# A written order placed anew: the last w_out quarter is loaded ahead of the third batch's x

## The chip, the cores and the metric

The kernel runs on one core of a Trainium2 chip. The metric is the device time of one execution in microseconds (us). Of the kernel before there are three timed runs and one further execution with the hardware profiler, whose trace is read here. In the profile the engines are PE (matrix engine; PEld is its weight load), DVE (vector), ACT (scalar), POOL (GpSimd) and SP (sync, which here only issues DMAs). Each engine works through its own queue in order.

## The reference, cut to what matters

There are 8 batches. Each has x of 8 heads, 512 tokens and depth 64, and a state of 8 heads, 32 rows and depth 64. Two softmax reads are made of the same scores, and their rows go through a two-layer net with a PReLU between.

```
scores = scale * x @ state.T            # [512, 32] per batch and head
xread  = softmax(scores) @ state        # each token reads the states
sread  = softmax(scale * state @ x.T) @ x   # each state row reads the tokens
rows   = concat(xread, sread), heads side by side     # [8 * 544, 512]
h      = rows @ w_in                    # w_in [512, 2048]
g      = max(h, 0) + alpha * min(h, 0)
out    = g @ w_out                      # w_out [2048, 512]
```

## The kernel before, in words

The two matmuls for xread are merged: state @ w_in is formed first (`m`, 32 steps), and h is the softmax weights times that product. So xread itself is never written.

The order of all work on all engines is one list of steps, ORDER (lines 17 to 102). Line 603 goes through the list, and each step appends its instructions to the queues of its engines. A step's letters name it, then follow batch, index, buffer or engine (a = ACT, v = DVE, p = POOL). The steps that the change and the prediction speak of are these:

- `lx.b` (line 162): POOL issues the load of batch b's x into one of four buffers xg. `lx0.g` loads half of batch 0. `lst` loads the states.
- `wi.f` (line 197) and `wo.i` (line 203): POOL issues the load of a quarter of w_in or w_out, 512 KB as written. All these loads turn float32 into float16 and share one software DMA queue.
- `xt`, `xo`: x of batches 0 and 1 is transposed on PE and copied out. `xd.b` (line 269): from batch 2 on, SP issues a DMA transpose of x, from xg to xT; SP waits for the landing of `lx.b` first. `str`, `sro`: states transposed and copied out.
- `sc.b` (line 291): scores on PE, 16 small matmuls, from xT into the PSUM buffer "two". `sb`, `smax`, `ssh`, `sexp`, `ssum`, `snorm`, `wb`: the softmax over states, on DVE, DVE, POOL, ACT, DVE, POOL and DVE; `wb.b` gives the weights aT.
- `tm`, `te`, `tsum`, `tn.b.g`, `tt.b`: the softmax over tokens, on DVE, ACT, DVE, POOL, and a DMA transpose issued by SP. `rd.b`: the state reads on PE, 32 small matmuls that read xg.
- `m.b.f`: state of batch b times w_in quarter f on PE (8 matmuls), into "two", or into two PSUM banks if two numbers follow. `mo`: its two copies to SBUF.
- `F.b.j.k`: h of column block j (16 of them) on PE, two matmuls of 512 columns into PSUM bank k; `f` is one of the two alone. It reads aT and the `m` of quarter j / 4. `N.b.j`: ACT forms max(-h, 0). `G.b.j`: DVE forms g from N and h, and frees the bank. `F.8` stands for the state reads of all batches, four matmuls of 256 columns.
- `S.b.q.i`: two of the 16 matmuls of an output tile q, with g of blocks 2i and 2i + 1; a last number is the PSUM bank. It needs w_out quarter i / 2. `O.b.q.e`: copy out and the store, issued by SP. `R`, `RO`, `L`, `LO` are the same for the state rows and for the last tile, cut into three pieces.
- `Z.k.n`: n matmuls of zeros, whose result is not used.

Of the kernel before, what the change touches and what calls it, by code (L numbers as in the profile page):

```python
# [42 lines left out]
O.1.2.a lx.4 mo.2.2.a.1 sb.3 N.2.15 S.1.0.1 tm.3 F.2.13.3 N.2.13 G.2.15 S.1.0.2 F.2.4.2 tn.2.0
F.2.2.4 G.2.13 smax.3 N.2.4 F.2.9.5 F.2.0.1 N.2.9 S.1.0.3 S.1.0.4 G.2.9 S.1.0.5 N.2.2 N.2.0 te.3.0
F.2.12.3 S.1.0.6 N.2.12 G.2.2 G.2.4 G.2.0 xd.4 F.2.7.5 G.2.12 S.1.3.0.4 ssh.p.3 sexp.3 N.2.7 ssum.3
S.1.0.7 te.3.1 F.2.3.2 S.1.3.1 F.2.1.1 N.2.3 S.1.3.2 N.2.1 F.2.8.3 G.2.3 S.1.3.3 G.2.1 S.1.3.4
S.1.3.5 N.2.8 S.1.3.6 G.2.7 F.2.6.2 O.1.0.a N.2.6 m.3.3.1.0 G.2.8 sc.4 rd.1.5 snorm.p.3 F.2.5.3
G.2.6 mo.3.3.a.0 F.2.14.1 rdo.1.a wb.3 N.2.5 tsum.3 S.2.1.0.2 F.2.11.5 mo.3.3.a.1 G.2.5 S.1.3.7
N.2.14 F.2.10.0 F.3.4.3 G.2.14 N.2.11 S.2.1.1 F.3.1.1 lx.5 O.1.3.v N.3.4 S.2.1.2 N.2.10 G.2.11 tt.2
S.2.0.0.4 S.2.1.3 S.2.0.1 G.2.10 F.3.14.5 F.3.9.0 S.2.1.4 tn.3.1 N.3.1 N.3.9 G.3.1 S.2.1.5 S.2.0.2  # L50
G.3.4 tn.3.0 N.3.14 tm.4 F.3.3.1 F.3.8.3 G.3.14 N.3.8 G.3.9 S.2.1.6 S.2.1.7 S.2.0.3 S.2.3.0.5 N.3.3
xd.5 O.2.1.a tt.3 sb.4 G.3.8 smax.4 F.3.6.0 F.3.2.2 te.4.0 S.2.3.1 S.2.3.2 N.3.6 N.3.2 F.3.13.3
S.2.0.4 te.4.1 ssh.p.4 N.3.13 G.3.3 G.3.6 S.2.0.5 F.3.7.1 G.3.2 S.2.0.6 N.3.7 S.2.0.7 sexp.4 G.3.13
G.3.7 S.2.3.3 S.2.3.4 S.2.3.5 m.6.0 O.2.0.v m.5.1.0.2 mo.6.0.a.1 mo.5.1.a.1 rd.3.3 mo.6.0.v.0
rdo.3.a mo.5.1.v.0 rd.2.1 m.4.1.4.2 ssum.4 sc.5 m.4.3.0.3 rdo.2.a S.2.3.6 mo.4.1.a.1 mo.4.1.a.0 tm.5
tsum.4 snorm.p.4 F.3.5.1 mo.4.3.a.0 mo.4.3.a.1 F.3.0.2 F.3.10.4 N.3.0 S.2.3.7 O.2.3.a S.2.2.0.0
S.2.2.1 F.3.11.3 G.3.0 wb.4 S.2.2.2 S.3.3.0.5 F.3.15.2 S.3.3.1 N.3.5 lx.6 G.3.5 te.5.0 te.5.1 N.3.10
N.3.15 S.2.2.3 F.3.12.1 S.2.2.4 N.3.11 S.3.3.2 lx.7 N.3.12 G.3.10 G.3.15 F.4.6.4 N.4.6 tn.4.0
F.4.5.2 G.3.11 F.4.3.3 N.4.5 S.2.2.5 G.3.12 G.4.5 S.3.3.3 F.4.4.1 S.3.3.4 F.4.7.2 N.4.4 S.3.3.5
S.2.2.6 N.4.3 sb.5 N.4.7 S.3.3.6 S.2.2.7 G.4.4 G.4.7 S.3.3.7 F.4.1.1 F.4.0.2 xd.6 O.2.2.a S.3.1.0.0  # L60
O.3.3.a S.3.1.1 F.4.9.5 N.4.1 smax.5 G.4.6 N.4.0 S.3.0.0.4 tn.4.1 S.3.0.1 G.4.1 G.4.0 F.4.8.1
S.3.1.2 tsum.5 N.4.9 ssh.p.5 G.4.3 sexp.5 N.4.8 G.4.9 F.4.11.2 F.4.2.3 N.4.2 S.3.0.2 ssum.5 S.3.0.3
S.3.0.4 tt.4 N.4.11 S.3.1.3 G.4.8 S.3.1.4 S.3.1.5 G.4.2 S.3.1.6 snorm.p.5 m.5.0.5.1 G.4.11 sc.6
m.5.3.3.2 xd.7 wb.5 mo.5.0.a.1 sb.6 S.3.1.7 mo.5.3.a.0 mo.5.0.a.0 F.4.13.1 N.4.13 S.3.0.5 mo.5.3.a.1
S.3.2.0.3 tm.6 S.3.0.6 te.6.0 F.4.10.5 F.5.3.2 smax.6 S.3.2.1 N.4.10 N.5.3 S.3.2.2 S.3.2.3 S.3.0.7
S.3.2.4 S.3.2.5 S.3.2.6 ssh.p.6 G.4.13 O.3.1.a tn.5.0 F.4.14.1 te.6.1 O.3.0.v S.3.2.7 G.4.10 G.5.3
N.4.14 F.4.12.0 G.4.14 O.3.2.a sexp.6 tn.5.1 S.4.1.0.4 m.6.3 m.7.2.5.2 m.5.2.3.1 mo.6.3.v.0 S.4.1.1
mo.5.2.v.0 mo.7.2.a.0 S.4.1.2 mo.5.2.a.1 F.5.15.5 mo.6.3.v.1 mo.7.2.a.1 tt.5 S.4.1.3 N.5.15 G.5.15
F.4.15.3 F.5.12.1 S.4.1.4 F.5.5.2 N.4.12 F.5.13.5 S.4.1.5 N.5.12 N.4.15 G.4.12 tsum.6 G.4.15
S.4.0.0.0 S.4.1.6 S.4.1.7 N.5.5 S.4.0.1 S.4.2.0.3 O.4.1.v G.5.5 S.4.0.2 F.5.10.4 N.5.13 F.5.1.2  # L70
S.4.2.1 G.5.12 F.5.0.1 N.5.10 S.4.0.3 S.4.2.2 S.4.0.4 G.5.13 tn.6.1 N.5.0 G.5.10 N.5.1 G.5.1
m.6.1.5.4 m.7.0 mo.6.1.a.1 mo.6.1.a.0 S.4.0.5 mo.7.0.v.0 S.4.0.6 F.5.2.2 N.5.2 S.4.0.7 mo.7.0.v.1
G.5.0 O.4.0.a rd.4.4 rd.5.5 G.5.2 m.7.3.1.0 rdo.4.a m.6.2.2.4 sc.7 rdo.5.a ssum.6 mo.7.3.a.0
mo.6.2.a.0 snorm.p.6 tn.6.0 S.4.3.0.5 S.4.3.1 mo.7.3.v.1 F.5.11.1 S.4.3.2 sb.7 S.4.3.3 N.5.11 G.5.11
F.5.6.2 F.5.9.0 S.4.2.3 S.4.2.4 F.5.7.1 S.4.3.4 mo.6.2.a.1 F.5.8.4 smax.7 S.4.3.5 S.4.3.6 wb.6
S.4.3.7 S.4.2.5 N.5.9 N.5.8 N.5.7 G.5.9 O.4.3.a G.5.8 F.5.4.0 N.5.4 tt.6 S.5.0.0.4 S.5.2.0.5 S.4.2.6
G.5.7 G.5.4 F.5.14.1 S.5.2.1 tm.7 S.5.0.1 N.5.6 S.4.2.7 F.6.3.0 N.5.14 G.5.6 S.5.2.2 S.5.0.2 te.7.1
F.6.15.2 N.6.3 G.6.3 S.5.2.3 N.6.15 S.5.2.4 S.5.0.3 G.6.15 ssh.p.7 S.5.2.5 F.6.7.0 S.5.1.0.2 N.6.7
S.5.0.4 G.5.14 O.4.2.v S.5.1.1 F.6.6.1 G.6.7 F.6.8.3 te.7.0 S.5.1.2 N.6.6 S.5.1.3 sexp.7 F.6.1.0
tsum.7 N.6.8 N.6.1 G.6.6 S.5.2.6 F.6.0.1 S.5.0.5 tn.7.1 tn.7.0 S.5.0.6 G.6.8 S.5.2.7 F.6.10.3 tt.7  # L80
N.6.0 S.5.1.4 G.6.1 S.5.1.5 S.5.1.6 S.5.1.7 F.6.14.0 N.6.10 O.5.1.a ssum.7 G.6.10 S.5.0.7 F.6.5.3
snorm.p.7 F.6.2.2 N.6.14 N.6.5 G.6.0 S.5.3.0.1 O.5.0.v G.6.14 m.7.1 G.6.5 rd.7.4 rd.6.0 rdo.7.v
N.6.2 O.5.2.a F.6.13.3 S.5.3.1 mo.7.1.v.0 rdo.6.a S.5.3.2 S.5.3.3 mo.7.1.v.1 F.6.9.5 F.8.4.4 N.6.9
G.6.2 S.5.3.4 wb.7 F.6.12.0 G.6.9 F.6.4.2 N.6.13 N.6.12 S.5.3.5 G.6.12 N.6.4 S.5.3.6 S.5.3.7
S.6.0.0.5 S.6.0.1 N.8.4 F.6.11.0 G.6.13 G.6.4 F.8.10.3 N.6.11 S.6.0.2 N.8.10 O.5.3.v G.8.4 S.6.1.0.2
F.7.0.1 S.6.0.3 F.7.7.4 N.7.0 S.6.1.1 G.6.11 S.6.0.4 N.7.7 S.6.0.5 G.7.0 S.6.1.2 F.8.14.0 S.6.1.3
S.6.1.4 G.8.10 S.6.0.6 N.8.14 F.7.3.1 S.6.0.7 G.7.7 S.6.1.5 F.8.3.3 F.7.6.4 G.8.14 N.7.3 F.8.2.0
O.6.0.v G.7.3 F.7.2.5 F.8.9.1 S.6.1.6 N.8.3 G.8.3 S.6.2.0.3 N.8.2 N.7.2 S.6.2.1 G.8.2 S.6.2.2 N.7.6
# [547 lines left out]
```

## Time and profile before

| what | value |
|---|---|
| three timed runs | 218.6, 218.71, 219.0 us, median 218.71 |
| profiled execution, its own time | 219.66 us |
| its span, first to last instruction | 217.9 us |
| mean granted clock of PE in it | 1.000 |
| PE busy | 210.6 us, 97% of the span |
| DVE busy | 165.2 us, 76% |
| ACT busy | 137.4 us, 63% |
| POOL busy | 71.0 us, 33% |
| software DMA queue (the loads) | 8.62 MB |
| hardware DMA queue (transposes and stores) | 14.23 MB |

A group line of the profile gives line, engine, operation, what is written from what, the count, then the busy time and mean duration, then the idle time of the engine ahead of the group and what ended it. A line of the timeline gives the start in us from the span's start, the duration, the engine and the operation; the bracket tells of idle time just before. "DMA to landing" is the time from a DMA's issue to the signal that all of it has arrived. Matmuls overlap, so one that lasts 379 ns starts 216 ns after the one ahead of it.

### The profile page before, as it was taken

How to read it: one execution, taken by the hardware profiler on the slowest of the kernel's cores; microseconds unless marked ns; L12 is line 12 of the kernel's file. 1: busy time of each engine (PE TensorE's matmuls, PEld its weight loads, DVE VectorE, ACT ScalarE, POOL GpSimd, SP SyncE). 2: the span in 40 equal slices, each digit the busy share in tenths (PEclk: the TensorE clock that was granted, in tenths of full speed). 3: DMA queues.
4: the chain of work that ended last, by engine and by line, in shares of the span. 5: the costliest groups of instructions: out<-in, count | busy, mean ns of one | idle time of the engine just before them, and what ended most of it. 6: DMA issues, size and time to landing. Idle time of an engine off the chain costs nothing.

```text
span 217.9 us, 4311 instructions
## 1 busy us (share of the span) xinstructions
PE 210.6 (97%) x1698; PEld 104.2 (48%) x1698; DVE 165.2 (76%) x250; ACT 137.4 (63%) x271; POOL 71.0 (33%) x58
## 2 busy tenths in 40 slices
...
GB/s 69 188 199 206 200 171 117 206 196 113 92 143 100 92 245 101 51 88 187 249 55 99 96 48 53 0 99 48 50 148 3 46 48 51 48 33 15 51 96 144
DMA packets 41748, 23.12 MB, mean 106 GB/s; under 512 B 24192, under 2 KB 38016, under 8 KB 41728
## 3 DMA queue, kind: packets, MB, share of 16 engines
q0 software_dynamic: 12704, 8.62, 28.5%
q1 hardware_dynamic: 26960, 14.23, 27.7%
q10 hardware_dynamic: 2064, 0.01, 0.5%
q8 instruction: 13, 0.21, 0.4%
q14 instruction: 7, 0.06, 0.1%
...
## 4 chain that ended last, share of the span: by engine, by line
PE 84%; DMA 9%; DVE 3%; POOL 1%; issue 1%; ACT 0%; POOLq 0%
PE o L526 47%; PE h L474 23%; DMA xT<-xg 4%; DMA w_in_sb<-in_moe_w_in_dram 3%; PE m_ps L441 3%; PE h L483 3%; PE o L574 3%; DMA xg<-in_x_dram 2%; PE o L546 2%; PE sr_ps L416 2%; PE sc L291 1%; POOL an L352 1%; DVE ts L326 1%; DVE m L463 1%; DVE mx L332 1%
## 5 line engine op out<-in xcount | busy, mean ns | idle before, releaser
L526 PE MATMUL o<-w_out_sb,gt 128*128 128x512 f16 x496 | 125.3, 379 | 0.9 <-DMA w_out_sb<-in_moe_w_out_dram 0.9
L506 ACT ACTIVATE neg<-h 128x512 f32<-128x512 f32 (+1 forms) x144 | 77.1, 579 | 47.8 <-PE h L474 38.4
L514 DVE SCALAR_TENSOR_TENSOR gt<-neg,oma_sb,h 128x512 f16<-128x512 f32 x128 | 89.9, 738 | 16.5 <-ACT neg L506 15.6
L526 PEld LDWEIGHTS <-gt 128*128 128x128 f16 x496 | 47.3, 98 | 56.4 <-issue 4.5
L474 PE MATMUL h<-aT,m 128*128 128x512 f16 x250 | 68.3, 379 | 0.0
L474 PEld LDWEIGHTS <-m 128*128 128x128 f16 x250 | 24.1, 98 | 28.4 <-issue 0.6
L397 POOL TENSOR_SCALAR e<-e,r 128x512 f16<-128x512 f16 x16 | 25.0, 1566 | 20.4 <-DVE r L393 16.6
L463 ACT CAST m<-m_ps 128x512 f16<-128x512 f32 x50 | 27.1, 606 | 4.6 <-PE m_ps L441 4.3
L352 POOL TENSOR_TENSOR an<-ts,r 128x1024 f16<-128x1024 f32 (+1 forms) x9 | 15.4, 1719 | 33.2 <-DVE r L349 14.8
L338 POOL TENSOR_TENSOR ts<-ts,mx 128x1024 f32<-128x1024 f32 (+1 forms) x9 | 15.5, 1720 | 30.9 <-DVE mx L332 30.9
L564 ACT COPY osb<-o 128x512 f32<-128x512 f32 x22 | 12.9, 591 | 14.9 <-PE o L526 14.9
L441 PE MATMUL m_ps<-w_in_sb,stT 64*32 64x512 f16 x256 | 11.3, 383 | 0.6 <-DMA w_in_sb<-in_moe_w_in_dram 0.4
L383 ACT ACTIVATE e<-sc,nb 128x512 f16<-128x512 f32 x16 | 11.1, 700 | 1.1 <-DVE nb L375 1.1
L360 DVE STREAM_TRANSPOSE aT<-an 128x1024 f16<-128x1024 f16 (+1 forms) x9 | 10.1, 1120 | 1.9 <-POOL an L352 1.9
L514 DVE SCALAR_TENSOR_TENSOR gs<-neg,oma_sb,h 128x256 f16<-128x256 f32 x16 | 7.5, 476 | 4.5 <-ACT neg L506 4.5
L463 DVE CAST m<-m_ps 128x512 f16<-128x512 f32 x14 | 9.1, 679 | 2.0 <-ACT m L463 1.6
L372 DVE TENSOR_REDUCE nb<-sc 128x2 f32<-128x1024 f32 x8 | 9.6, 1202 | 0.5 <-PE sc L291 0.5
L332 DVE TENSOR_REDUCE mx<-ts 128x32 f32<-128x1024 f32 (+1 forms) x9 | 9.8, 1091 | 0.0
L348 DVE TENSOR_REDUCE r<-ts 128x32 f32<-128x1024 f32 (+1 forms) x9 | 9.8, 1087 | 0.0
L483 PE MATMUL h<-XS,w_in_sb 128*128 128x256 f16 x64 | 9.4, 273 | 0.0
L584 DVE COPY osr<-o 128x512 f32<-128x512 f32 x1 | 0.7, 692 | 11.3 <-PE o L574 11.3
L344 ACT ACTIVATE ts<-ts 128x1024 f32<-128x1024 f32 (+1 forms) x9 | 8.6, 960 | 0.2 <-POOL ts L338 0.2
...
## 6 DMA issues: line engine op xcount, KB each, us to landing
...
```

Source lines behind the costliest of these rows:

```text
L332: nc.vector.tensor_reduce(cols(live["mx", b], j, S // N), blocks(cols(live["ts", b], j, S)), AX.X, ALU.max)
L338: engine(e).tensor_tensor(ts, ts, over_blocks(cols(live["mx", b], j, S // N)), ALU.subtract)
L352: engine(e).tensor_tensor(blocks(cols(live["an", b], j, S)), blocks(cols(live["ts", b], j, S)), over_blocks(cols(live["r1", b], j, S // N) ...
L397: nc.gpsimd.tensor_scalar_mul(e2, e2, live["r2", b][:, g : g + 1])
L441: nc.tensor.matmul(t[N * k : N * (k + 1), :], st_head(b, h)[64 * r : 64 * r + 64, :], w_in_sb[64 * r : 64 * r + 64, c, 512 * f : 512 * (f ...
L463: copier(e)(m_tile(b)[:, f, g, :], live["mp", b, f][g])
L474: nc.tensor.matmul(h.rearrange("p (r j s) -> p r j s", r=2, j=2), ms[b][:, f, g, 128 * j : 128 * (j + 1)], weights(b, g), start=(g == 0), ...
L483: nc.tensor.matmul(h, w_in_sb[:, c, 128 * jc : 128 * (jc + 1)], XS[:, c].rearrange("p q n b -> p (q n b)"), start=(c == 0), stop=(c == n_c ...
L506: nc.scalar.activation(neg, h, RELU, bias=0.0, scale=-1.0)
L514: nc.vector.scalar_tensor_tensor(gt, negs.pop((b, jc)), oma_sb[:, jc : jc + 1], h, ALU.mult, ALU.add)
L526: nc.tensor.matmul(outs[b, q], gts[b, jc][:, 128 * q : 128 * (q + 1)], w_out_sb[:, jc, :], start=(jc == 0), stop=(jc == n_jc - 1),)
L564: copier(e)(osb, t)
```

## The change

Only the list ORDER is replaced; the step functions stay as they are. The head of both lists is shown, to the scores of batch 3.

```diff
--- before.py
+++ after.py
@@ -15,90 +15,90 @@
 ORDER = """
-stc lx0.0 lx0.1 oma id Z.1.20 stt.0 Z.2.18 xt.0.0.0.1 sto.a xt.0.1.0.2 xo.0.0.0.v lst xo.0.1.0.v
-Z.0.6 sc.0.0 xt.0.1.1.3 xt.0.0.1.4 sb.0.0 xo.0.0.1.v smax.0.0 xo.0.1.1.a str.0.5 sc.0.1 str.1.0 wi.0
-sro.0.a lx.1 wi.1 ssh.p.0.0 sb.0.1 Z.1.3 sc.0 Z.5.7 m.0.0.1.2 sro.1.a sexp.0.0 smax.0.1 m.3.0.3.4
-ssh.p.0.1 tm.0 mo.0.0.a.1 sexp.0.1 ssum.0.0 m.1.0.5.0 ssum.0.1 te.0.1 te.0.0 mo.1.0.v.1 wo.0
-mo.1.0.a.0 snorm.p.0.0 mo.3.0.a.1 Z.2.28 xt.1.1.1.2 xt.1.1.0.5 mo.0.0.a.0 snorm.p.0.1 wb.0.0
-mo.3.0.a.0 m.2.0 xt.1.0.1.0 xo.1.1.0.v xt.1.0.0.4 f.0.0.0.1 f.0.1.0.5 wi.2 mo.2.0.a.0 wb.0.1
-mo.2.0.a.1 f.0.1.1 xo.1.0.0.v N.0.1 m.0.1.3.4 f.0.0.1 mo.0.1.a.1 m.1.1 xo.1.1.1.v N.0.0 xo.1.0.1.v
-mo.0.1.v.0 f.0.2.0.2 F.0.3.0 f.0.2.1 F.0.4.3 mo.1.1.v.0 mo.1.1.a.1 F.0.7.4 G.0.1 N.0.2 G.0.0 wo.1
-F.0.5.5 N.0.3 G.0.2 wi.3 m.4.0 N.0.4 S.0.0.0.1 N.0.5 G.0.3 tsum.0 S.0.1.0.2 N.0.7 mo.4.0.a.1 G.0.4
-S.0.0.1 S.0.1.1 G.0.5 mo.4.0.a.0 tn.0.1 m.0.2.0.3 sc.1 G.0.7 S.0.2.0.5 mo.0.2.a.0 tm.1 m.1.2.0.4
-wo.2 tn.0.0 mo.0.2.a.1 mo.1.2.a.0 S.0.2.1 lx.2 sb.1 F.0.6.3 F.0.9.0 mo.1.2.a.1 N.0.6 S.0.2.2 S.0.0.2
-N.0.9 G.0.6 S.0.1.2 smax.1 te.1.1 te.1.0 F.0.11.4 G.0.9 ssh.p.1 F.0.8.3 wo.3 N.0.8 N.0.11 S.0.0.3
-S.0.1.3 m.0.3 G.0.8 F.0.10.0 mo.0.3.a.0 N.0.10 sexp.1 S.0.2.3 mo.0.3.v.1 xd.2 G.0.11 G.0.10
-S.0.3.0.3 m.1.3 S.0.3.1 mo.1.3.a.0 F.0.14.4 S.0.2.4 F.0.13.0 N.0.14 tt.0 ssum.1 S.0.0.4 S.0.1.4
-S.0.0.5 S.0.3.2 G.0.14 F.0.12.4 N.0.13 G.0.13 F.0.15.0 snorm.p.1 N.0.12 N.0.15 mo.1.3.a.1 wb.1
-S.0.3.3 S.0.1.5 S.0.3.4 G.0.12 S.0.2.5 G.0.15 S.0.3.5 F.1.2.4 S.0.2.6 N.1.2 F.1.0.0 tsum.1 S.0.2.7
-N.1.0 S.0.1.6 S.0.1.7 G.1.2 O.0.2.a sc.2 m.2.1.4.5 S.0.0.6 O.0.1.a F.1.7.2 mo.2.1.a.0 mo.2.1.a.1
-G.1.0 F.1.1.0 tm.2 sb.2 F.1.3.4 N.1.7 S.0.0.7 S.0.3.6 N.1.1 G.1.1 N.1.3 tn.1.0 O.0.0.a te.2.0
-F.1.5.5 S.0.3.7 N.1.5 G.1.3 F.1.9.0 S.1.1.0.1 G.1.7 F.1.4.4 smax.2 O.0.3.a S.1.1.1 tn.1.1 G.1.5
-rd.0.2 te.2.1 N.1.9 G.1.9 m.2.3 F.1.6.3 N.1.4 rdo.0.a F.1.12.5 N.1.6 lx.3 G.1.4 F.1.13.2 N.1.12
-F.1.8.0 G.1.6 G.1.12 S.1.2.0.4 N.1.13 G.1.13 ssh.p.2 N.1.8 S.1.1.2 F.1.11.3 G.1.8 F.1.10.5 N.1.11
-S.1.2.1 N.1.10 G.1.11 G.1.10 S.1.2.2 sexp.2 S.1.1.3 ssum.2 F.1.14.2 F.1.15.0 snorm.p.2 mo.2.3.a.0
-S.1.1.4 mo.2.3.a.1 S.1.1.5 m.3.2 m.4.2.3.5 N.1.14 tt.1 tsum.2 N.1.15 G.1.14 mo.3.2.a.1 S.1.1.6
-S.1.2.3 S.1.2.4 mo.3.2.a.0 mo.4.2.a.0 G.1.15 mo.4.2.a.1 S.1.2.5 S.1.1.7 xd.3 O.1.1.a m.3.1.2.0
-m.2.2.3.5 sc.3 wb.2 tn.2.1 S.1.2.6 S.1.2.7 mo.3.1.a.1 F.2.15.1 S.1.0.0.0 mo.2.2.a.0 mo.3.1.a.0
...
+lx0.0 stc lx0.1 id oma Z.1.20 stt.0 lst Z.2.18 xt.0.1.0.1 xt.0.0.0.2 sto.v wi.0 xo.0.1.0.a
+xo.0.0.0.v Z.0.6 sc.0.0 xt.0.1.1.3 sb.0.0 xt.0.0.1.4 xo.0.1.1.a lx.1 xo.0.0.1.v str.1.5 smax.0.0
+sc.0.1 str.0.0 sro.1.a sb.0.1 wi.1 Z.1.3 sc.0 Z.5.7 m.0.0.1.2 sro.0.a smax.0.1 ssh.p.0.0 ssh.p.0.1
+wi.2 sexp.0.0 mo.0.0.a.0 tm.0 ssum.0.0 sexp.0.1 mo.0.0.v.1 m.3.0.3.4 snorm.p.0.0 mo.3.0.a.1 ssum.0.1
+m.1.0.5.0 Z.1.18 m.4.0.1.4 mo.1.0.v.1 wb.0.0 mo.3.0.a.0 te.0.1 m.2.0.2.3 mo.4.0.a.1 Z.0.10
+xt.1.0.1.4 xt.1.1.1.0 mo.2.0.a.0 mo.1.0.v.0 wo.0 mo.4.0.a.0 snorm.p.0.1 xt.1.0.0.2 xt.1.1.0.1 wb.0.1
+te.0.0 f.0.2.0.5 xo.1.1.1.a xo.1.0.1.v mo.2.0.a.1 m.0.1 F.0.3.0 f.0.0.0.4 mo.0.1.a.1 f.0.0.1
+f.0.1.0.3 tsum.0 mo.0.1.v.0 xo.1.0.0.v xo.1.1.0.v N.0.3 N.0.0 f.0.1.1 wo.1 f.0.2.1 wi.3 F.0.7.2
+F.0.5.1 N.0.1 tn.0.1 wo.2 tn.0.0 m.0.2 N.0.2 G.0.3 G.0.0 N.0.7 N.0.5 F.0.4.0 mo.0.2.a.0 F.0.6.4
+G.0.1 G.0.7 m.1.2.3.2 mo.0.2.a.1 N.0.6 sc.1 G.0.5 N.0.4 F.0.9.1 wo.3 mo.1.2.a.1 G.0.2 S.0.1.0.5
+G.0.6 mo.1.2.a.0 S.0.1.1 m.1.1.4.2 N.0.9 G.0.4 F.0.10.3 S.0.3.0.0 mo.1.1.a.0 S.0.3.1 F.0.11.4 sb.1
+S.0.1.2 S.0.1.3 tm.1 N.0.10 mo.1.1.a.1 smax.1 N.0.11 te.1.0 S.0.2.0.2 ssh.p.1 S.0.3.2 G.0.10 S.0.3.3
+S.0.2.1 te.1.1 m.0.3 mo.0.3.a.1 G.0.11 F.0.8.3 mo.0.3.v.0 S.0.2.2 N.0.8 S.0.2.3 G.0.9 G.0.8 F.0.14.4
+F.0.13.1 sexp.1 F.0.12.3 N.0.13 S.0.2.4 lx.2 S.0.1.4 N.0.12 S.0.1.5 S.0.2.5 S.0.3.4 N.0.14 ssum.1
+G.0.12 snorm.p.1 xd.2 G.0.13 G.0.14 S.0.3.5 F.0.15.3 N.0.15 tt.0 S.0.3.6 m.2.1.1.4 m.1.3 mo.2.1.a.1
+mo.1.3.a.0 mo.1.3.a.1 wb.1 G.0.15 S.0.2.6 S.0.1.6 F.1.7.4 mo.2.1.v.0 S.0.1.7 S.0.3.7 F.1.13.3
+F.1.3.1 N.1.7 S.0.2.7 O.0.3.a tsum.1 F.1.4.0 O.0.1.v F.1.1.5 G.1.7 N.1.13 G.1.13 N.1.3 S.0.0.0.4
+G.1.3 N.1.4 O.0.2.a F.1.5.3 F.1.0.1 N.1.1 G.1.4 N.1.5 S.0.0.1 G.1.1 F.1.2.2 N.1.0 S.0.0.2 sc.2
+m.3.1.0.5 G.1.5 S.0.0.3 N.1.2 mo.3.1.a.1 mo.3.1.a.0 G.1.0 F.1.6.3 N.1.6 sb.2 S.0.0.4 tn.1.1 S.0.0.5
+S.0.0.6 G.1.2 S.0.0.7 F.1.10.1 tm.2 F.1.11.5 tn.1.0 smax.2 O.0.0.a S.1.2.0.0 N.1.10 G.1.6 S.1.1.0.2
+F.1.9.4 S.1.2.1 N.1.11 te.2.1 te.2.0 S.1.1.1 S.1.1.2 F.1.8.3 G.1.11 tsum.2 N.1.9 G.1.10 S.1.2.2 lx.3
+S.1.1.3 G.1.9 m.3.2.5.1 m.2.3 xd.3 N.1.8 F.1.12.4 ssh.p.2 sexp.2 S.1.2.3 mo.2.3.a.1 G.1.8 N.1.12
+mo.3.2.v.0 mo.2.3.a.0 F.1.14.3 tt.1 S.1.1.4 mo.3.2.a.1 ssum.2 F.1.15.5 N.1.14 S.1.2.4 S.1.2.5
+S.1.1.5 G.1.12 S.1.2.6 N.1.15 G.1.14 m.2.2.1.4 sc.3 G.1.15 snorm.p.2 mo.2.2.a.0 rd.0.3 rd.1.5 wb.2
+rdo.0.a mo.2.2.a.1 S.1.1.6 F.2.15.1 tm.3 rdo.1.a S.1.2.7 sb.3 O.1.2.a F.2.2.3 S.1.1.7 F.2.13.4 N.2.2
...
 """
```

As queues, the changes that the prediction uses are these. POOL, before and after, from the second load of w_in to the third batch's softmax:

```
before: wi.1 ssh.0.0 ssh.0.1 wo.0 snorm.0.0 snorm.0.1 wi.2 wo.1 wi.3 tn.0.1 wo.2
        tn.0.0 lx.2 ssh.1 wo.3 snorm.1 tn.1.0 tn.1.1 lx.3 ssh.2 snorm.2 tn.2.1 lx.4
after:  wi.1 ssh.0.0 ssh.0.1 wi.2 snorm.0.0 wo.0 snorm.0.1 wo.1 wi.3 tn.0.1 wo.2
        tn.0.0 wo.3 ssh.1 lx.2 snorm.1 tn.1.1 tn.1.0 lx.3 ssh.2 snorm.2 lx.4 ssh.3
```

SP, from its first transpose to the fifth batch's:

```
before: xd.2 tt.0 O.0.2 O.0.1 O.0.0 O.0.3 tt.1 xd.3 O.1.1 O.1.2 xd.4
after:  xd.2 tt.0 O.0.3 O.0.1 O.0.2 O.0.0 xd.3 tt.1 O.1.2 O.1.1 xd.4
```

The 28 zero matmuls of `Z.2.28` become `Z.1.18` and `Z.0.10`; 82 stay in all. PE's queue holds the same steps in another order and in other PSUM banks, except that from `F.7.2` on, in the last fifth, the order of PE is the same and only banks differ. The reads `rd.0` move behind `sc.3`, where `rd.1` follows them. `lx.7` stands ahead of `lx.6`. One shift of the state softmax, `ssh` of batch 7, goes from POOL to DVE; the first copy `sto` goes from ACT to DVE, and some copies trade ACT for DVE or back.

118 lines of the change are left out of this document (59 added, 59 removed).

## The prediction

> **What bounds the kernel now.** I read the page first: busy times and the chain that ended last.
>
> ```profile
> span 217.9 us, 4311 instructions
> PE 210.6 (97%) x1698; PEld 104.2 (48%) x1698; DVE 165.2 (76%) x250; ACT 137.4 (63%) x271; POOL 71.0 (33%) x58
> PE 84%; DMA 9%; DVE 3%; POOL 1%; issue 1%; ACT 0%; POOLq 0%
> ```
>
> PE works nearly without a break, so the time is PE's matmuls plus its gaps, and a change of order can only move gaps. The 9% of DMA on the chain show where to look. The chain in order of time names the two places:
>
> ```profile
> 15.75 7.17 DMA w_in_sb<-in_moe_w_in_dram
> ...
> 33.71 7.65 DMA xT<-xg
> ```
>
> Next come the waits of the whole run, the timeline around 30 to 42 us, and the landing times of the two kinds of transpose (of x first, of the token weights second):
>
> ```profile
> PE o L526 <- DMA w_out_sb<-in_moe_w_out_dram: 0.9, 1, 0.9
> PEld L291 <- DMA xT<-xg: 0.6, 1, 0.6
> ```
> ```profile
> 25.90 0.94 POOL L162 DMA_DIRECT2D xg<-in_x_dram  x1
> 28.12 1.91 POOL L338 TENSOR_TENSOR ts<-ts,mx 128x1024 f32<-128x1024 f32 x1 [1.28 <-DVE mx L332]
> 29.98 0.79 POOL L203 DMA_DIRECT2D w_out_sb<-in_moe_w_out_dram  x1
> 33.71 4.85 SPq L269 DMA_TRANSPOSE xT<-xg  x1
> ```
> ```profile
> 38.97 0.59 PE L526 MATMUL o<-w_out_sb,gt 128*128 128x512 f16 x2 [0.85 <-DMA w_out_sb<-in_moe_w_out_dram]
> ```
> ```profile
> DMA to landing us min/median/max: 3.7/4.3/7.7
> ```
> ```profile
> DMA to landing us min/median/max: 3.0/3.4/6.9
> ```
>
> So `wo.3`, issued at 29.98, lands 8.9 us later (its own row), at 38.9, and PE stands still 0.85 us for it. `xd.2`, issued at 33.71 beside it, takes 7.65 us where the best of its kind take 3.7, and `sc.2` starts at 41.41, just behind its landing. The table of stretches shows both crawling together (columns: stretch; length, busy us of five engines, clock, DMA share, GB/s):
>
> ```profile
> 34.00:35.50 1.50, 1.50 (x9) 0.69 (x7) 0.69 (x2) 0.32 (x1) 1.50 (x1) 1.00 1.18 193
> 35.50:38.50 3.00, 2.62 (x13) 1.08 (x11) 2.61 (x4) 1.59 (x4) 0.25 (x2) 1.00 1.43 39
> 38.50:41.50 3.00, 2.41 (x18) 0.97 (x25) 1.50 (x2) 1.50 (x4) 3.00 (x3) 1.00 1.11 219
> ```
>
> The DMA engines count as occupied from 35.5 to 38.5 but move 39 GB/s instead of some 200. The other slow transpose, 6.9 us, is `tt.1`, issued at 47.2 with `lx.3` still landing.
>
> **The change, part by part.** *Loads.* From 4 to 34 us the loads move at a steady 172 to 203 GB/s, one after another, and every quarter is issued 3 us or more before its turn. So a load's landing belongs to its place in the queue. The landings from the second w_in quarter's place on are 17.2, 19.8, 22.9, 25.1, 27.6, 31.0, 33.6 (issue plus landing rows). Before, places two to seven hold `wo.0 wi.2 wo.1 wi.3 wo.2 lx.2`; after, `wi.2 wo.0 wo.1 wi.3 wo.2 wo.3`. So `wi.2` comes at 19.8 (3.1 earlier), `wo.0` at 22.9 (3.1 later), `wo.3` at 33.6 (5.3 earlier). `lx.2` is last: some 2.6 us (the step between places) behind, 36.4. Its issue stands behind `ssh.1`, which ends about 30.1, and adds 0.9 us on POOL ahead of `snorm.1`; that is hidden, since `ssum.1` ends about 33.
>
> *The transpose.* `xd.2` starts at 36.5 with no load in flight, at 3.7 us: 40.2. Its bounds are 3.7 and 7.65; I take 3.7 because three of the six landed in 3.7 with no load beside them. `tt.0` and the first stores queue behind it on SP and lose nothing: the first store is due at 39.1.
>
> *PE.* I count PE's work to a checkpoint by starts: 0.216 us for a 512-column matmul (eight from 32.78 to 34.51), so 0.43 for an F or S, 0.24 for `sc`, 0.225 for `m`, 0.6 for `rd`, and 0.2 for each change from large matmuls to 64x32 ones and back (0.1 either way at 41.97). Start time minus work ahead gives the lag, in which all gaps are gathered (changes included).
>
> Up to `m.0.1` both orders wait for the w_in quarter of 17.2, and start it at 17.28. The changed one has 0.21 us less work behind it then, since `Z.0.10` must wait for the bank that `mo.1.0.v.1` clears at 15.5 (DVE: `mo.0.0.v.1`, 0.63, now stands between the two `ssum`, and pushes it from 14.96).
>
> Then, by hand along the queues (DVE starts a G each 0.665 us, ACT an N or `mo` each 0.48):
> - `m.0.2` starts at 20.1, with `wi.2` there; the gap of 0.17 at 22.96 goes.
> - Late next is `m.1.2`: its bank 2 waits for `G.0.7`, the fourth G after 19.1, at 21.8. Gap 0.5.
> - `sc.1` waits for "two", emptied by `mo.0.2.a.1` at 22.4. Gap 0.5. It starts at 22.48 with 14.06 us of work ahead: lag 8.42. Before, 23.21 and 15.35: lag 7.86. So the change is 0.56 behind here.
> - `S.0.1.0` at 23.25 finds `wo.0` landed at 22.9; had it stayed ahead of it, this would be the next wait.
> - `m.0.3` at 28.9 ("two" free at 28.5), `F.0.12` waits 0.15 to 0.2 for `G.0.8` at 31.5, `S.0.3.6` at 35.0 finds `wo.3` of 33.6 there, `F.1.7` at 37.0 finds `wb.1` done at 36.3. No other gap.
> - `sc.2` starts at 43.1 with 33.73 us ahead: lag 9.37. Before: 41.41 and 31.35, lag 10.06. `xT` has been there since 40.2.
>
> That is 0.69 us ahead. From `sc.2` on, the order before has 10 changes of matmul size, the new one 11: 0.2 given back. Further on before has one gap of 0.2 (at `m.4.3`, 90.7), and following the new queues to 94 us I find one of about 0.15 (`S.2.2.0`, for `mo.4.3.a.0`). Those cancel. Moves between engines cost nothing while off PE's path: `ssh.7` on DVE adds at most the 1.91 of its POOL row, where `wb.7` has about 2 us in hand; without that it would show in full.
>
> Sum: 0.69 - 0.20 = 0.5 us less. Against its own span, 217.9 becomes 217.4. The profiled execution took 219.66, 1.76 more than its span and 0.95 more than the median of the runs, so I take the difference off the median: 218.71 - 0.5 = 218.2.
>
> **A rule against the trace.** The row is 7.65 us beside a load, 3.7 without. The Trainium skill, *DMA: Bandwidth & Descriptors* (Rules for kernel authors), says a transpose next to ordinary DMAs needs nothing; *Advanced Engine Details and Errata* (X-Bar Transpose) calls transposes as fast as regular DMAs. Read as a statement on speed, the first would leave 7.65 unexplained by the load and lasting after the change, which is the first rival below; by it the time would be 219.2. The rows of 39 GB/s and of `tt.1` speak against it.
>
> **The rivals.** *The transpose is slow for itself.* `xd.2` is the program's first transpose; if that is what costs, 36.5 + 7.65 = 44.15, and `sc.2` waits 1.05 from 43.1: 218.2 + 1.05 = 219.2, slower. Against it: `tt.1`, no first one, takes 6.9 beside a load.
>
> *The reads come too early (the slower side).* `rd.1` stood at 71.6 and now stands at 56.8, right behind `sc.3` and `rd.0`. Its `tt.1` is now behind `xd.3` on SP, which waits for `lx.3` (issued about 40.8) and for `O.0.0` (about 47.5). With `xd.3` at 47.7 and 3.2 of issue, `tt.1` goes out at 51 to 52 and lands at 3.4 more by 55.5: in time by 1.3. With the 6.9 that it took before, 58.9: 2.1 late, 220.3. It decides from a landing of 4.8. `F.2.15` at 57.8 has only 0.15 in hand to `wb.2`, so smaller gaps, to 0.5, stand here too. Also `lx.4` now waits for `rd.0` with `ssh.3` behind it on POOL; `smax.3` comes only at 62, so this is covered.
>
> *The two gaps of 0.5 at 21.5 to 22.5 don't come*, as when DVE runs ahead: 217.2.
>
> *The gaps in the head grow*, `wo.0` landing later than its place says, say by 0.5: 218.7, no change.
>
> **How the numbers follow.** No change is a difference within 0.2% (0.44 us), about what a measurement tells. Forecast as worked out, own range 217.9 to 218.6: 0.40, of it 0.27 faster and 0.13 same. Gaps don't come: 0.15, faster. Gaps grow: 0.15, 0.12 same and 0.03 slower. Reads too early or other new gaps behind 43 us: 0.22, all but 0.01 slower. Transpose slow for itself: 0.08, 0.02 same and 0.06 slower. Sums: faster 0.42, same 0.28, slower 0.30. The range for 8 in 10 goes from 217.2, the gaps not coming, to 219.8, inside the late reads.
>
> **What would show it.** Right: `w_out` no longer ends a wait of PE; `xd.2` lands in about 3.7, `sc.2` starts near 43.1 with no wait for xT; `sc.1` starts near 22.5 behind a gap. Wrong: `xd.2` above 6 us; PE waiting for e2T at `rd.1` near 57; gaps at `F.2.15`, or behind 94 us, where I did not follow the queues.

## The result, and the profile after

The changed kernel is slower. Beside the first runs the kernel before took 218.86 us (median of 6) and the changed one 220.49 (6 runs, 220.3 to 220.62): a ratio of 1.0070, 95% interval 1.0053 to 1.0087. In a later set of runs, on one chip, the two stood at 218.69 and 220.59, 1.0076 (1.0050 to 1.0102). One timed run of those below, 223.07 us at a granted clock of 0.991, is a slow one and is left out. The prediction was 218.2 us with a range of 217.2 to 219.8, so both the sign and the range missed.

The profiled execution took 220.3 us, 1.8 more than its span. Its page, with the busy times and the chain that ended last:

```profile
span 218.5 us, 4306 instructions
PE 210.3 (96%) x1698; PEld 102.9 (47%) x1698; DVE 162.8 (75%) x248; ACT 139.3 (64%) x274; POOL 69.2 (32%) x57
PE 80%; DVE 6%; ACT 6%; DMA 5%; issue 1%; POOL 1%; POOLq 0%; ACTq 0%
```

DMA has gone from 9% of the chain to 5%, as was meant. DVE and ACT have come in its place, from 3% and 0% to 6% each. PE has no more work than before (210.3 us busy against 210.6), so the new time is new idle time.

The place that the change aimed at looks as forecast. In the timeline of SP and POOL, the load of the third x goes out at 30.17 and its transpose at 36.11. The view of the tile xT shows that the slow transposes of x are gone: the first one took 4.02 us in its own row, and the longest 5.4 (of the token weights the longest took 5.0 instead of 6.9). In the groups, the output matmuls (L526) now have no idle time ahead of them at all.

```profile
30.17 0.92 POOL L162 DMA_DIRECT2D xg<-in_x_dram  x1
36.11 1.87 SPq L269 DMA_TRANSPOSE xT<-xg  x1
```
```profile
DMA to landing us min/median/max: 3.7/3.9/5.4
```
```profile
L526 PE MATMUL o<-w_out_sb,gt 128*128 128x512 f16 x496 | 124.5, 379 | 0.0
```

`xd.2` landed at 40.13 and `sc.2` began at 43.78 without a wait for it. But the forecast had it begin at 43.1. What made it late stands in the waits of the whole run: the DVE copies of `m` (L463) waited 2.7 us for copies of the same line on ACT (1.6 in the kernel before).

```profile
DVE m L463 <- ACT m L463: 2.7, 3, 1.3
```

The kernel before has the same kind of wait. The line of its waits, and three rows of its timeline:

```profile
DVE m L463 <- ACT m L463: 1.6, 2, 1.2
```
```profile
17.73 1.39 DVE L463 CAST m<-m_ps 128x512 f16<-128x512 f32 x2 [0.17 <-PE m_ps L441]
17.83 0.66 ACT L463 CAST m<-m_ps 128x512 f16<-128x512 f32 x1
29.95 0.69 DVE L463 CAST m<-m_ps 128x512 f16<-128x512 f32 x1 [0.42 <-ACT m L463]
```

Before, `m.0.1` goes into two separate banks, and its halves are copied side by side, from 17.73 and 17.83. The three products that go into the two-bank buffer "two" and are copied out by both engines (`m.1.1`, `m.0.3`, `m.6.0`) are copied one half after the other; the row at 29.95 is `m.0.3`. The change puts `m.0.1` into "two" as well.

The timeline of the changed kernel shows where the first two of its three waits sit and what hangs on them (brackets: idle time just before, and what ended it):

```profile
18.01 0.69 DVE L463 CAST m<-m_ps 128x512 f16<-128x512 f32 x1 [0.77 <-ACT m L463]
18.62 0.74 DVE L282 COPY xT<-xT_ps 128x512 f16<-128x512 f16 x2
19.09 1.04 PE L474 MATMUL h<-aT,m 128*128 128x512 f16 x4 [0.20 <-DVE xT L282]
```
```profile
29.56 0.59 ACT L463 CAST m<-m_ps 128x512 f16<-128x512 f32 x1 [0.98 <-PE m_ps L441]
30.18 0.69 DVE L463 CAST m<-m_ps 128x512 f16<-128x512 f32 x1 [0.65 <-ACT m L463]
30.79 1.40 DVE L514 SCALAR_TENSOR_TENSOR gt<-neg,oma_sb,h 128x512 f16<-128x512 f32 x2
30.93 1.90 PE L474 MATMUL h<-aT,m 128*128 128x512 f16 x6
```

`mo.0.1.v.0`, the DVE half of a copy out of the two-bank buffer "two", begins at 18.01, just when ACT's half `mo.0.1.a.1` ends, though PE had filled both by 17.3. The copies of `xt` behind it clear the bank of `F.0.7`, which waits. At 30.18 the same happens to `mo.0.3.v.0` behind `mo.0.3.a.1` (29.56 to 30.15). `G.0.9` and `G.0.8` stand behind it on DVE. They free the banks of `F.0.13` and `F.0.12`, so the six matmuls of `F.0.14`, `F.0.13` and `F.0.12` take 1.90 us.

Three more gaps stand behind 91 us:

```profile
89.48 1.89 DVE L463 CAST m<-m_ps 128x512 f16<-128x512 f32 x3 [1.30 <-ACT m L463]
91.42 0.40 PE L441 MATMUL m_ps<-w_in_sb,stT 64*32 64x512 f16 x4
91.75 1.47 PE L526 MATMUL o<-w_out_sb,gt 128*128 128x512 f16 x6
119.17 0.59 PE L474 MATMUL h<-aT,m 128*128 128x512 f16 x2 [0.34 <-ACT osb L564]
120.92 1.21 DVE L332 TENSOR_REDUCE mx<-ts 128x32 f32<-128x1024 f32 x1
122.11 0.73 DVE L514 SCALAR_TENSOR_TENSOR gt<-neg,oma_sb,h 128x512 f16<-128x512 f32 x1
122.89 0.59 PE L474 MATMUL h<-aT,m 128*128 128x512 f16 x2
```

The first comes from the third such copy, `mo.6.0.v.1`, which waits for `mo.6.0.a.0`. It pushes the two DVE copies behind it, `mo.5.1.v.1` and `mo.4.2.v.1`, which clear banks for `m.4.3` and `m.4.1`. The last four matmuls of `m.4.1` start at 91.42, just behind the last of these copies (89.48 + 1.89 = 91.37), and `S.2.3.7` follows them at 91.75. The second is `F.5.0` at 119.17: its bank is cleared by `O.3.0`, which the change gives to ACT. The third is `F.5.13` at 122.89: its bank is cleared by `G.5.0` at 122.11, which stands on DVE behind the 1.21 us of `smax.6`.

### The profile page after: what moved, and what is told of

Same layout as the page of the kernel before. It is cut to its first block, busy times and chain, and to the rows that moved or that the text cites. A ratio compares the mean times of both kernels' runs of the same rounds, so it can differ in the third digit from the quotient of the medians.

```text
span 218.5 us, 4306 instructions
## 1 busy us (share of the span) xinstructions
PE 210.3 (96%) x1698; PEld 102.9 (47%) x1698; DVE 162.8 (75%) x248; ACT 139.3 (64%) x274; POOL 69.2 (32%) x57
## 4 chain that ended last, share of the span: by engine, by line
PE 80%; DVE 6%; ACT 6%; DMA 5%; issue 1%; POOL 1%; POOLq 0%; ACTq 0%
PE o L526 45%; PE h L474 21%; DVE gt L514 4%; PE h L483 3%; PE o L574 3%; PE m_ps L441 3%; DMA e2T<-e 2%; DMA st<-in_state_dram 2%; PE sr_ps L416 2%; ACT m L463 2%; PE o L546 2%; ACT e L383 1%; ACT stT L259 1%; DVE m L463 1%; ACT neg L506 1%
## 5 line engine op out<-in xcount | busy, mean ns | idle before, releaser
L526 PE MATMUL o<-w_out_sb,gt 128*128 128x512 f16 x496 | 124.5, 379 | 0.0
L506 ACT ACTIVATE neg<-h 128x512 f32<-128x512 f32 (+1 forms) x144 | 78.4, 582 | 42.0 <-PE h L474 34.0
L526 PEld LDWEIGHTS <-gt 128*128 128x128 f16 x496 | 47.8, 98 | 55.9 <-issue 2.8
L474 PE MATMUL h<-aT,m 128*128 128x512 f16 x250 | 69.2, 379 | 0.8 <-ACT osb L564 0.3
L474 PEld LDWEIGHTS <-m 128*128 128x128 f16 x250 | 23.6, 98 | 31.1 <-issue 4.2
L463 ACT CAST m<-m_ps 128x512 f16<-128x512 f32 x50 | 27.8, 604 | 5.5 <-PE m_ps L441 5.5
L564 ACT COPY osb<-o 128x512 f32<-128x512 f32 x24 | 14.1, 588 | 18.3 <-PE o L526 18.3
L338 POOL TENSOR_TENSOR ts<-ts,mx 128x1024 f32<-128x1024 f32 (+1 forms) x8 | 13.6, 1694 | 36.0 <-DVE mx L332 28.5
L463 DVE CAST m<-m_ps 128x512 f16<-128x512 f32 x14 | 9.2, 676 | 3.9 <-ACT m L463 2.7
L216 PE MATMUL z<-zero 128*128 128x128 f16 x82 | 6.9, 245 | 2.2 <-DVE zero L210 1.0
```

The costliest lines, as they stand in the source:

```text
L338: engine(e).tensor_tensor(ts, ts, over_blocks(cols(live["mx", b], j, S // N)), ALU.subtract)
L463: copier(e)(m_tile(b)[:, f, g, :], live["mp", b, f][g])
L474: nc.tensor.matmul(h.rearrange("p (r j s) -> p r j s", r=2, j=2), ms[b][:, f, g, 128 * j : 128 * (j + 1)], weights(b, g), start=(g == 0), ...
L506: nc.scalar.activation(neg, h, RELU, bias=0.0, scale=-1.0)
L526: nc.tensor.matmul(outs[b, q], gts[b, jc][:, 128 * q : 128 * (q + 1)], w_out_sb[:, jc, :], start=(jc == 0), stop=(jc == n_jc - 1),)
L564: copier(e)(osb, t)
```

## The experiments

To put numbers of different runs side by side, I used the prediction's lag again: the start of a PE step less the nominal work ahead of it (here with 0.2 us for each change of matmul size counted as work). It gathers all gaps. These are its increases in us by stretch, from one profiled execution each. The names stand for the kernels below, in their order there: c_before is the kernel before once more, e2_swap and e2_again the exchange of the two loads, e2b_front the exchange with both loads ahead, e6_cover the covered waits; c_after is the changed kernel once more, e3_unswap the exchange back, e1_fill the two copies moved, e7_tail the tail repaired, e5_late and e5_again both.

```
             up to m.0.1   m.0.1-m.1.3   m.1.3-sc.2   sc.2-last piece
before           5.73          0.49         1.23          0.71
c_before         6.02          0.51         0.61          0.72
e2_swap          6.30          0.96         0.67          0.72
e2_again         6.18          0.49         1.40          0.72
e2b_front        6.01          0.50         0.03          0.72
e6_cover         5.93          0.50         0.73          0.87
after            5.52          2.11         0.02          1.15
c_after          5.70          2.05         0.02          1.17
e3_unswap        6.48          2.68         0.02          1.13
e1_fill          6.32          1.03         0.02          1.02
e7_tail          5.73          2.11         0.02          0.33
e5_late          5.87          1.00         0.03          0.33
e5_again         5.87          1.01         0.02          0.33
```

(The wait for the last w_out quarter falls into the third column in the old order and, where there is one, into the second in the new.) The first column differs between executions of one and the same kernel too (5.73 and 6.02, 5.52 and 5.70). In most rows `m.0.1` starts just behind the landing of the second w_in quarter, which lies between 16.76 and 17.78 us; not in all: in c_before it landed at 17.07 and `m.0.1` started at 17.57. The diffs below show only the pieces of ORDER's lines that an experiment changes.

**The kernel before, once more.**

> The kernel before once more, with a profile. The profiled execution shown of it took 219.66 us, 0.8 over the median of the timed ones, and its first load of x landed at 6.5 us where the changed kernel's landed at 5.8. If that is the start of the loads in one execution and not the order, this one has a span near 217.1 us, a first PE transpose of x near 5.9 us, and ratio 1.000. If the order is what moves the first load, it shows 6.5 us and 217.9 us again.

It took 218.90 us, ratio 1.0001 (0.9978 to 1.0024). This profiled execution took 219.36 us. The same waits are there, but smaller:

```profile
PEld L291 <- DMA xT<-xg: 0.6, 1, 0.6
PE o L526 <- DMA w_out_sb<-in_moe_w_out_dram: 0.2, 1, 0.2
```
```profile
34.08 4.20 SPq L269 DMA_TRANSPOSE xT<-xg  x1
```

The last w_out quarter landed at 38.63 instead of 38.93, and `S.0.2.6` waited 0.2 instead of 0.85 us. So the 0.85 that I had set out to remove is not a fixed cost of this kernel. The start was not as expected: the first load of x came in nearly as late as in the first profile (6.33 us against 6.52). In all, 88 runs of the kernel before stood beside the experiments. They reach from 218.10 to 220.57 us; 26 of them lie above 219.3. Both its profiled executions, 219.66 and 219.36, belong to that upper part.

**The two late copies of the head moved behind work that doesn't wait (on the kernel after).**

```diff
-f.0.1.0.3 tsum.0 mo.0.1.v.0 xo.1.0.0.v xo.1.1.0.v N.0.3
+f.0.1.0.3 tsum.0 xo.1.0.0.v xo.1.1.0.v mo.0.1.v.0 N.0.3
...
-mo.0.3.a.1 G.0.11 F.0.8.3 mo.0.3.v.0 S.0.2.2 N.0.8 S.0.2.3 G.0.9 G.0.8
+mo.0.3.a.1 G.0.11 F.0.8.3 S.0.2.2 N.0.8 S.0.2.3 G.0.9 mo.0.3.v.0 G.0.8
```

> The changed kernel with two DVE copies moved a few places later in DVE's own queue (mo.0.1.v.0 behind the x copies, mo.0.3.v.0 behind G.0.9), so that DVE has work while ACT copies the other half of the same two-bank tile. No work is added or left out. Theory (a DVE copy waits for ACT's copy of the same tile, and that idle time reaches PE): the gaps of PE at F.0.7 (0.3 us), F.0.13 and F.0.12 (0.2 each) go, the one at F.0.14 stays: 0.7 us less than the changed kernel, 219.8 us, ratio to before 1.004. Rivals (the places of the loads, or the stretch behind 94 us, make the loss): no difference, 220.5 us, ratio 1.0075.

It took 219.78 us, ratio 1.0041 (1.0020 to 1.0062): 0.7 to 0.8 less than the changed kernel. Its waits and timeline:

```profile
DVE m L463 <- ACT m L463: 1.3, 1, 1.3
```
```profile
30.33 0.69 DVE L463 CAST m<-m_ps 128x512 f16<-128x512 f32 x1
31.08 1.47 PE L474 MATMUL h<-aT,m 128*128 128x512 f16 x6
```

Of the three waits one is left, the one at 89.5. The copy at 30.33 stands behind `G.0.9` without an idle moment, the six h matmuls take 1.47 us instead of 1.90, and the gaps at `F.0.7`, `S.0.1.0`, `F.0.13` and `F.0.12` are gone; the one of 0.2 at `F.0.14` stays, as expected. The second column of the table falls by 1.0 to 1.1 us. In this one execution the first column is 0.6 to 0.8 higher than in the two of the changed kernel, so the size is better read from a later pair of runs.

**Only the exchange of the two loads, in the old order.**

```diff
-S.0.2.1 lx.2 sb.1 F.0.6.3
+S.0.2.1 wo.3 sb.1 F.0.6.3
...
-ssh.p.1 F.0.8.3 wo.3 N.0.8 N.0.11
+ssh.p.1 F.0.8.3 lx.2 N.0.8 N.0.11
```

> The kernel before with one exchange in POOL's queue alone: wo.3 and lx.2 trade places, all else stays. Theory (a load in flight is what makes the transpose and the load crawl): wo.3 lands near 33.6, lx.2 near 36.3, the transpose takes about 4 us and ends near 40.3, PE's wait of 0.85 us at S.0.2.6 goes and sc.2 is reached about 40.4 with at most 0.1 us to wait: 1.0 us less than before, 217.9 us, ratio 0.9955. Rival (the first transpose of a program is slow by itself): it ends at 44 us, sc.2 waits 3.5 us, 221.5 us, ratio 1.012. Rival (the gap moves elsewhere): ratio 1.000.

> The exchange of wo.3 and lx.2 alone once more, for a second profile. In the first one batch 1's x landed at 15.7 us against 14.0 and 14.3 in two profiles of the kernel before, ahead of anything that the exchange touches, and sc.2 then waited some 0.55 us for xT. If the late x is chance, it lands near 14.2 here, PE reaches sc.2 about 40.5, and the whole loss stands as one wait for xT, which ends 4 us after lx.2's landing of 37 to 38: a gap of 1 us or more at sc.2. If the late x belongs to this kernel, it lands at 15.7 again and the gap at sc.2 stays near 0.5. Time as before this run: 220.1 us, ratio 1.006.

The same kernel gave 220.06 us, ratio 1.0062 (1.0037 to 1.0088), and on another chip 219.11 (nine runs), ratio 1.0005 (0.9980 to 1.0030). Neither is the gain I expected, and the two intervals exclude each other, so a difference of 0.5% between sets of runs can't be read as this order's own. The traces agree on why nothing is gained. The wait for xT and the transpose in SP's timeline of the first of the two, then the wait in the second:

```profile
PEld L291 <- DMA xT<-xg: 1.1, 1, 1.1
```
```profile
37.87 1.76 SPq L269 DMA_TRANSPOSE xT<-xg  x1
```
```profile
PEld L291 <- DMA xT<-xg: 1.8, 1, 1.8
```

The transposes are quick (3.97 and 3.95 us), but x goes out behind `ssh.1` at 30.5, lands at 37.8 and 37.9, and xT is there at 41.8 and 42.0, later than the crawling transpose had it (41.36 and 41.05). The wait for w_out became a wait for xT, because `sc.2` stands some 2.4 us earlier in the old order than in the new. Batch 1's x, which the second run was to settle, landed at 15.19 us there, between the two values expected, and at 15.0 and 15.35 in the next two orders, which have the same head. So a late x isn't this kernel's own.

**The exchange with both loads ahead of the shift `ssh.1`.**

```diff
-S.0.2.1 lx.2 sb.1 F.0.6.3
+S.0.2.1 wo.3 lx.2 sb.1 F.0.6.3
...
-ssh.p.1 F.0.8.3 wo.3 N.0.8 N.0.11
+ssh.p.1 F.0.8.3 N.0.8 N.0.11
```

> The kernel before with wo.3 and lx.2 exchanged and both issued ahead of ssh.1, so that x is issued near 27 us and not behind ssh.1 at 30.5. Theory (the exchange loses because x, last and issued late, lands at 37 to 38, so that a transpose of 4 us ends no sooner than the one of 7 to 7.7 that began at 33.7): lx.2 lands in its place, 36.3 to 36.8, xT is there at 40.3 to 40.8, and sc.2 waits 0.3 us at most: 218.8 us, ratio 0.999, about 1.2 us better than the plain exchange. Rival (the place behind ssh.1 does not matter): 220.0 us, ratio 1.006.

It took 218.90 us, ratio 0.9997 (0.9979 to 1.0015). In its trace x goes out at 26.99, the transpose begins at 35.65 with nothing in flight and takes 4.10, w_out is there at 32.90, and neither PE nor its weight loads wait for either. The whole cost of the place is gone (0.03 in the third column; the span is 217.0 us), and yet the time is that of the kernel before. So over many executions the two waits cost at most what the interval leaves, 0.46 us, not the 1.2 us (third column) of the profile that I had read.

```profile
26.99 0.89 POOL L162 DMA_DIRECT2D xg<-in_x_dram  x1
35.65 1.84 SPq L269 DMA_TRANSPOSE xT<-xg  x1
```

**The waits covered by work instead of removed (on the kernel before).**

```diff
-F.1.2.4 S.0.2.6 N.1.2 F.1.0.0 tsum.1
+F.1.2.4 F.1.0.0 S.0.2.6 N.1.2 tsum.1
...
-O.0.2.a sc.2 m.2.1.4.5 S.0.0.6
+O.0.2.a S.0.0.6 sc.2 m.2.1.4.5
```

> The kernel before, loads as they were, with two exchanges in PE's queue: F.1.0 goes ahead of S.0.2.6, so that 0.43 us of work stands in front of the wait for wo.3, and S.0.0.6 goes ahead of sc.2, in front of the wait for xT. Theory (in a typical execution the wait for wo.3 is 0.4 us or more): 0.4 to 0.5 us less than before, 218.4 us, ratio 0.998. Rival (the wait of 0.85 us belongs to a slow execution and is near nothing in a typical one): no difference, ratio 1.000.

It took 219.05 us, ratio 1.0003 (0.9981 to 1.0025). No gain again, as the rival had it, but the test is weaker than planned. In its profiled execution (219.53 us) the waits are still there: the transpose crawled as ever (7.31 us, issued at 34.19), w_out landed at 39.09, past the 0.43 us of work put in front, `S.0.2.6` waited 0.2 us and the weight loads of `sc.2` 0.6, and the third column has 0.73.

**The two loads exchanged back, in the new order.**

```diff
-F.0.9.1 wo.3 mo.1.2.a.1 G.0.2
+F.0.9.1 lx.2 mo.1.2.a.1 G.0.2
...
-S.0.2.4 lx.2 S.0.1.4
+S.0.2.4 wo.3 S.0.1.4
```

> The changed kernel with the same exchange undone: lx.2 ahead of ssh.1, wo.3 behind it, all else as changed. Theory: the transpose starts near 33.2 with wo.3 in flight, takes about 7.5 us, and wo.3 lands near 38.5 while S.0.3.6 is due at 35.7: PE waits some 2.5 us, 223 us, ratio 1.019. Rival (load and transpose share the engines without a standstill): wo.3 lands by 36, no wait above 0.3 us, 220.5 us, ratio 1.0075.

It took 221.31 us (four runs), ratio 1.0112 (1.0079 to 1.0146), between what the two theories gave. Its SP and POOL timelines, the landings of its x transposes, and its waits:

```profile
31.09 0.79 POOL L203 DMA_DIRECT2D w_out_sb<-in_moe_w_out_dram  x1
33.22 3.91 SPq L269 DMA_TRANSPOSE xT<-xg  x1
```
```profile
DMA to landing us min/median/max: 3.7/3.8/8.7
```
```profile
PE o L526 <- DMA w_out_sb<-in_moe_w_out_dram: 0.5, 1, 0.5
```

With w_out in flight (31.09 to 37.18) the transpose took 8.73 us, the longest of all, and `S.0.3.6` waited 0.5 us for w_out. Nothing else of the order differs. So in both orders the exchange alone decides whether this transpose is quick or slow: a load beside it is what makes it slow. In the new order the exchange is worth about 0.8 us (221.31 against 220.5).

**The three gaps behind 91 us repaired as well, on top of the head's two copies.**

```diff
-lx.7 F.3.15.1 tsum.4 mo.6.0.v.1 S.2.3.6 mo.4.2.a.0 mo.5.1.v.1 mo.4.2.v.1
+lx.7 F.3.15.1 tsum.4 S.2.3.6 mo.4.2.a.0 mo.5.1.v.1 mo.6.0.v.1 mo.4.2.v.1
...
-G.4.14 N.4.2 O.3.0.a S.3.2.4
+G.4.14 N.4.2 O.3.0.v S.3.2.4
...
-S.4.0.0.3 smax.6 tn.5.1 F.4.15.5 N.5.3 O.3.2.a S.4.1.1 ssh.p.6 tsum.6 G.5.0
+S.4.0.0.3 G.5.0 smax.6 tn.5.1 F.4.15.5 N.5.3 O.3.2.a S.4.1.1 ssh.p.6 tsum.6
```

> The changed kernel with the two DVE copies moved as before, and three more moves that leave no work out: mo.5.1.v.1 goes ahead of mo.6.0.v.1 (which waits for ACT), the copy O.3.0 goes from ACT to DVE, and G.5.0 goes ahead of smax.6. They aim at the three gaps of PE behind sc.2: 0.35 us near 91.5, 0.34 at F.5.0, 0.28 at F.5.13. Theory (the rest of the loss is these gaps): 0.7 to 0.9 us less than with the two copies alone, 219.0 us, ratio 1.0005. Rival (the gaps only move to the next late instruction): 219.8 us, ratio 1.004.

It took 218.72 us, ratio 0.9990 (0.9975 to 1.0006), 1.06 us under the two copies alone, which ran in another set.

**The last set: the changed kernel, the repair of its tail alone, and the repair of both, on one chip.**

> The changed kernel again, as the measure for the two runs beside it. If the order's own gaps make the difference, it repeats: 220.5 us, ratio to the kernel before 1.007. If chance of the day made it (the same exchanged order gave 1.006 in one set of runs and 1.0005 in another), the ratio is below 1.004.

> The changed kernel with only the three gaps behind 91 us repaired, and the head left as the change has it. Theory (the gaps of head and tail add up, the tail's share being 219.78 - 218.72 = 1.06 us as the two runs stood): 1.06 under the changed kernel beside it, 219.4 us, ratio 1.002. Rival (the tail's trace shows only 0.7 us of lag saved, the rest was spread between runs): 0.7 under it, 219.8 us, ratio 1.004. If a gain of the head is needed for the tail's to show, the ratio stays at 1.007.

> The changed kernel with the two late copies of the head and the three gaps behind 91 us repaired, once more. Theory: 218.7 us, ratio to before 0.999, and 1.8 us under the changed kernel beside it. Rival (it only fell in a good set of runs): 219.5 or more, ratio above 1.002.

They took 220.59 (ratio 1.0076, 1.0050 to 1.0102), 219.87 (1.0044, 1.0026 to 1.0061) and 218.72 us (0.9994, 0.9976 to 1.0012). So the difference of the changed kernel is its own and repeats. The tail's three gaps are worth 220.59 - 219.87 = 0.72 us; the trace says 1.17 - 0.33 = 0.84 (the rival's size was the right one). The three moves were made together. In the trace the second and third gap are gone, while the first is only made smaller: from `m.6.0` to `S.2.3.7` it is 3.21 us (88.59 to 91.80) instead of 3.37 (88.38 to 91.75). The head's two copies are worth 219.87 - 218.72 = 1.15 us; the trace says 2.11 - 1.01 = 1.10. Together 1.87 us, all that the change had lost. The page of the repaired kernel (first run) and the wait that is left in it (its six h matmuls take 1.47 us):

```profile
span 216.9 us, 4307 instructions
PE 90%; ACT 5%; DMA 2%; issue 1%; POOL 1%; POOLq 0%
```
```profile
DVE m L463 <- ACT m L463: 0.2, 1, 0.2
```

DVE is gone from the chain. This is the best version of the new order. It isn't shown to beat the kernel before, whose ratio of 1 lies in both intervals. It is steadier: of its 24 timed runs one lies above 219.3 us, of the 88 of the kernel before 26.

## Why the prediction was wrong, and where it was right

**Right.** *Loads*: the w_in quarter forecast for 19.8 landed at 19.30, `wo.0` at 22.05 (22.9), `wo.3` at 32.21 (33.6), `lx.2` at 36.02 (36.4): each place a little early, none late. *The transpose*: 3.7 forecast, 4.02 measured, against 7.65 beside a load. Across the runs it took 3.94 to 4.10 us in the nine executions where no load was in flight and 6.98 to 8.73 in the four where one was. The rival that the first transpose is slow for itself falls with that. `tt.1`, which the prediction held against it, would not have settled it: it took 6.9 us in that one execution, 4.2 to 4.5 in the five others of the old order beside the same load, and 3.15 to 4.94 in the seven of the new order with no load in flight. The Trainium skill says that a transpose next to ordinary DMAs needs nothing (*DMA: Bandwidth & Descriptors*, Rules for kernel authors) and that transposes are as fast as regular DMAs (*Advanced Engine Details and Errata*, X-Bar Transpose). Read as statements on speed beside a load, the traces don't agree: here the load cost the first transpose 3 to 5 us. *The removed waits*: both are gone, `sc.2` no longer waits. *The gaps ahead of `sc.1`*: forecast 1.0 us in two, measured 0.77 in one row. That `sc.1` began at 22.38 (22.48) is partly luck: `m.0.1` began 0.4 early, and a gap of 0.37 that I didn't have, at `F.0.7` (18.51 to 19.09, of which 0.216 is work), took most of that back. *The reads*: `rd.1` found its weights there and `F.2.15` had no gap, so that rival did not come. The margin of 0.9 us is partly luck: `tt.1` took 4.9 us instead of 3.4 and landed at 56.5, but `rd.1` itself came 0.6 late, at 57.4. The rival of two gaps that don't come did not either.

**Wrong, first step: the walk by hand behind `sc.1`, "no other gap".** From `sc.1` to `sc.2` I had 20.62 us and it took 21.40, 0.78 more. The trace has four gaps there, 0.85 us in all: 0.20 at `S.0.1.0`, and 0.20, 0.22 and 0.23 at `F.0.14`, `F.0.13` and `F.0.12`. I had one, of 0.15 to 0.2. The gap at `F.0.7`, ahead of `sc.1`, comes on top. What I had missed is a wait between two engines: of a copy out of "two" in halves, the second listed half begins only when the first ends, `mo.0.3.v.0` at 30.18. My walk has no such wait. It let `G.0.8`, which stands behind that half on DVE, clear the bank of `F.0.12` at 31.5; in the trace `G.0.8` ends at 32.2. The profile of the kernel before showed the wait, 1.6 us in its list, and the walk doesn't carry it over to `m.0.1` and `m.0.3` of the new order. The cost of 1.1 us was shown by taking it away (1.15 us less time). It also takes back the gain: `sc.2` began at 43.78, a lag, in the prediction's count, of 43.78 - 33.73 = 10.05, where before had 10.06. The 0.69 us were gone before they could be passed on.

**Wrong, second step: "those cancel".** I followed the queues to 94 us and took the rest as even, with 0.2 given back behind `sc.2`. From equal lags at `sc.2` the span ended 0.6 us behind. Three gaps were there, one inside the stretch I had followed, again a half copy that waits for the other half, and two behind it. The second of the three contradicts a sentence of the prediction, that moves between engines cost nothing while off PE's path: `O.3.0`, moved from DVE to ACT, came onto it, and `F.5.0` waited 0.34 us. With the three moves against them the time fell by 0.72 us. That new gaps could stand behind 94 us was named as what would make the prediction wrong, but it had no term in the sum.

**Wrong, third step: taking "the difference off the median".** The two profiles differ by 220.3 - 219.66 = 0.64 us, the medians by 1.6 to 1.9. I had said that the profiled execution lay 0.95 above the median and then used its waits as if every execution had them. The run with the waits removed and nothing changed in PE's order (0.9997) shows that there was hardly anything to gain, at most 0.46 us by its interval. The run meant to cover them (1.0003) agrees but proves less, since its profile still has them. What the 0.85 us wait is in a typical execution was not seen, since both profiles of that kernel were of its longer executions; the second shows 0.2.

So the miss of 220.5 - 218.2 = 2.3 us is about 0.7 from the walk to `sc.2`, 0.4 more than forecast behind it, and about 1 from the base; the rest, 0.2, is less than sets of runs differ.

**Open.** Why the load of the third x, issued last of the group, took 5.85 to 6.0 us in the three executions with the head as the change has it, 7.4 to 7.5 in the three with the head's copies moved, and 7.2 and 7.5 in the old order with the exchange. Why the exchange alone gave 1.0062 in one set and 1.0005 in another. And the gap of 0.7 us at `sc.1`, which the repaired order still has: removing it was not tried.
